# A gated linear recurrence and its feed-forward block on one core: the order of emission taken from a list schedule, early chunks transposed on TensorE, weights loaded in pieces

## The chip, the cores and the metric

The kernel runs on one core of a Trainium2 chip. The metric is the device time of one execution in microseconds (us); lower is better. The core's engines run their own instruction queues in order: TensorE (PE: matmuls, and transposes as matmuls against an identity), VectorE (DVE), ScalarE (ACT: tanh, exp, sqrt and copies), GpSimd (POOL) and SyncE (SP: here it only issues transfers). The matmuls write to PSUM, which DVE and ACT read.

## What is computed

```python
sig_r, sig_i = sigmoid(r_gate), sigmoid(i_gate)                  # x, gates: (4, 5824, 256)
a_t = exp(8 * sig_r * log(clip(sigmoid(a_param), 1e-6, 1 - 1e-6)))
x_gated = sqrt(max(1 - a_t * a_t, 1e-6)) * sig_i * x
for t in range(5824):                                            # a recurrence along the sequence
    h = a_t[:, t] * h + x_gated[:, t]
    y[:, t] = h
y = y.reshape(23296, 256)
out = (((y @ w1) * (y @ w2)) @ w3) @ w_out                       # w1, w2: 256x1024, w3: 1024x1024, w_out: 1024x256
```

All inputs and the output are float32; matmuls run in bf16.

## The kernel before

The 23296 tokens are cut into 46 chunks: chunk 0 of 256 tokens, the others of 512. A chunk passes through a front, a scan and the matmuls.

- The front. `load` fetches r, i and x of the chunk (256 columns of float32, tokens on partitions; three buffers for each of the three). `tanh_r` and `tanh_i` run on ACT (a sigmoid is a tanh of half the argument). POOL makes u from th_i and x (L106, L107). The recurrence needs the channels on partitions, so th_r and u are transposed as bf16 by `turn`: one DMA transpose on SP's queue (two for chunk 0), tiles rt and ut. `decay` (ACT, L125, twice a chunk, one for each half of the 256 channels) makes a_t as an exp, `square` (POOL, L131) its square, `root` (ACT, L136) the norm, `gated` (DVE, L144) the gated input.
- The scan. `scan` (DVE, L164, twice a chunk) runs the recurrence, with the last column of the chunk before as its start; `cast` (POOL, L170) makes y_t in bf16.
- The matmuls. `up` computes, for two of the eight blocks of 128 features at a time, pa with w1 and pb with w2 (four matmuls each; a pool of three PSUM tiles "pab"), ACT copies pa to sa, DVE multiplies sa by pb into g_t. w3 and w_out are multiplied once into wp_sb: `fold` loads 128 rows of w3 by POOL's queue, transposes them on TensorE (ptw), copies them (w3t), multiplies by wo (pw) and copies the result. `down` multiplies 128 tokens of g_t by wp_sb into po, ACT copies two of these to ot, SP stores them. ptw, pw and po share two PSUM tiles, "po".

A tanh or an exp needs one table on ACT, the square root another; a change of table is an ACT_TABLE_LOAD. So the chunks are put in groups (1, 1, 2, 3, nine times 4, and 3): the roots of a group stand together.

The order is written by hand as a loop over steps s, one chunk each, with four quarters. In a quarter stand one `up` of chunk s, one `down` of chunk s - 2, a piece of the scan of chunk s + 2, and the operations of the fronts that a table `queue` spreads over the steps ahead. The eight folds stand in steps 0 and 1. Weights: w1, w2 and wo are asked for whole at the start on POOL's queue, each w3 block where its fold stands. No instruction is reordered after this: each engine takes its own in the order of emission and waits for what it needs.

Of the kernel before, what the change touches and what calls it, by code (L numbers as in the profile page):

```python
# [1 line left out]

# [16 lines left out]
def kernel(  # L19
# [12 lines left out]
    nc = tc.nc  # L32
# [50 lines left out]
    def load(c):  # L83
        n = sizes[c] // P
        for nm, src in (("r", rf), ("i", jf), ("x", xf)):
            t = loads.tile([P, 4, D], F32, name=nm + "_t", tag=nm)
            nc.sync.dma_start(  # L87
                out=t[:, :n, :],
                in_=src[starts[c]:starts[c] + sizes[c], :].rearrange("(n p) c -> p n c", p=P))
            T[nm, c] = t  # L90

    def tanh_r(c):
        n = sizes[c] // P
        t = gates.tile([P, NCB, 4, P], BF16, name="th_r", tag="th_r")
        nc.scalar.activation(out=t[:, :, :n, :].rearrange("p cb j q -> p j cb q"),  # L95
                             in_=T["r", c][:, :n, :].rearrange("p j (cb q) -> p j cb q", q=P),
                             func=AF.Tanh, scale=0.5)
        T["pr", c] = turn(t, n, "rt")
        T["a", c] = held.tile([P, NCB, CT], F32, name="a_t", tag="a")

    def tanh_i(c):
        n = sizes[c] // P
        t = gates.tile([P, 4, D], F32, name="th_i", tag="th_i")
        nc.scalar.activation(out=t[:, :n, :], in_=T["i", c][:, :n, :], func=AF.Tanh, scale=0.5)  # L104
        u = gates.tile([P, NCB, 4, P], BF16, name="u_t", tag="u")
        nc.gpsimd.tensor_scalar(t[:, :n, :], t[:, :n, :], 1.0, 0.5, op0=ALU.add, op1=ALU.mult)  # L106
        nc.gpsimd.tensor_mul(out=u[:, :, :n, :].rearrange("p cb j q -> p j cb q"),  # L107
                             in0=t[:, :n, :].rearrange("p j (cb q) -> p j cb q", q=P),
                             in1=T["x", c][:, :n, :].rearrange("p j (cb q) -> p j cb q", q=P))
        T["u", c] = u  # L110

    def turn(src, n, tag):
        dst = (gates if tag == "rt" else held).tile([P, NCB, 4, P], BF16, name=tag, tag=tag)
        if n == 4:
            nc.sync.dma_start_transpose(out=dst.rearrange("p cb j q -> p (cb j) q"),
                                        in_=src.rearrange("p cb j q -> p (cb j q)"))
        else:
            for cb in range(NCB):
                nc.sync.dma_start_transpose(out=dst[:, cb, :n, :],
                                            in_=src[:, cb, :n, :].rearrange("p j q -> p (j q)"))  # L120
        return dst.rearrange("p cb j q -> p cb (j q)")

    def decay(c, cb):
        w = sizes[c]
        nc.scalar.activation(out=T["a", c][:, cb, :w], in_=T["pr", c][:, cb, :w], func=AF.Exp,  # L125
                             scale=la4[:, cb:cb + 1], bias=la4[:, cb:cb + 1])
# [41 lines left out]
    def cast(c):  # L168
        w = sizes[c]
        nc.gpsimd.tensor_copy(out=T["y", c][:, :, :w], in_=T["h", c][:, :, :w])  # L170

    def up(c, mp):
# [159 lines left out]
```

## Time and profile before

| | |
|---|---|
| median of 3 runs | 600.25 us (599.87 to 605.09) |
| profiled execution | 604.79 us, its span (first to last instruction) 602.9 us |
| PE, DVE, ACT, POOL busy | 503.1, 459.5, 460.2, 360.1 us |
| DMA transposes | 47 for rt, 47 for ut |
| bytes read from and written to HBM | 78.91 MB, 23.86 MB |

Times in profile rows are us from the start of the span, unless marked ns. A timeline row has start, duration, engine, line, operation, output<-input, and in brackets the idle time before it with what ended it; SPq is the issue of a transfer by SP. A row by stages has, behind its bounds, the busy us of PE, PE's weight loads, DVE, ACT and POOL with their instruction counts, then the clock granted to TensorE, the busy share of the DMA engines and GB/s. A row of waits has the total, the number and the longest. q0 is the queue of transfers issued by POOL, q1 that of SP. Matmuls overlap, so their starts tell the pace better than their durations.

### The profile page before, as it was taken

The numbers are of one execution on the slowest core, as the hardware profiler recorded it, in microseconds if no ns is written. First come the engines' busy times: TensorE is split into PE (matmuls) and PEld (weight loads), VectorE is DVE, ScalarE is ACT, GpSimd is POOL, SyncE is SP. The second block draws the span as 40 slices with busy tenths as digits, with TensorE's granted clock in tenths as the row PEclk, the third lists the DMA queues.
The fourth block names the chain that finished last, engine by engine and source line by source line (L and its number), as shares of the span: only waits on it lengthen the run. The fifth ranks groups of instructions, "written<-read, shape, count | busy, mean of one in ns | idle before, by whom it ended". The sixth has DMA issues, their size and how long they took to land.

```text
span 602.9 us, 8389 instructions
## 1 busy us (share of the span) xinstructions
PE 503.1 (83%) x3056; PEld 302.3 (50%) x3056; DVE 459.5 (76%) x347; ACT 460.2 (76%) x537; POOL 360.1 (60%) x201
## 2 busy tenths in 40 slices
PE   0010826888899999999999999999999999999997
PEld 0000513444455565565555556556555555665565
DVE  0120333699799899999998998998998998988741
ACT  3466142698979989899899899889899898785443
POOL 3065281289497596595794893993993974630100
PEclk9999975999999999999999999999999999999999
DMA  9979588088989799789789999887998988421113
GB/s 195 292 210 251 128 204 184 2 219 194 307 205 315 222 195 336 213 192 339 203 196 313 210 209 307 210 241 252 223 272 228 215 221 268 99 77 49 40 53 106
DMA packets 196090, 123.51 MB, mean 205 GB/s; under 512 B 100304, under 2 KB 194512, under 8 KB 196048
## 3 DMA queue, kind: packets, MB, share of 16 engines
q1 hardware_dynamic: 193312, 119.30, 73.6%
q0 software_dynamic: 2736, 3.67, 3.8%
q8 instruction: 24, 0.39, 0.3%
q14 instruction: 18, 0.15, 0.1%
HBM read 78.91 MB, written 23.86 MB: 170 GB/s over the span
## 4 chain that ended last, share of the span: by engine, by line
PE 55%; ACT 12%; issue 11%; DVE 7%; POOL 7%; DMA 5%; SPq 3%; ACTq 0%; POOLq 0%; DVEq 0%
PE po L197 18%; PE pa L178 18%; PE pb L186 17%; ACT sa L181 5%; DVE g_t L190 5%; ACT a_t L125 3%; SPq L87 3%; POOL nrm L131 3%; DMA rt<-th_r 2%; POOL u_t L107 2%; DVE h_t L164 1%; DMA w_t<-in_moe_w_dram 1%; POOL th_i L106 1%; ACT th_i L104 1%; PE pw L220 1%
## 5 line engine op out<-in xcount | busy, mean ns | idle before, releaser
L190 DVE TENSOR_TENSOR g_t<-sa,pb 128x1024 bf16<-128x1024 bf16 (+1 forms) x184 | 218.3, 1195 | 67.4 <-ACT sa L181 55.5
L181 ACT CAST sa<-pa 128x1024 bf16<-128x1024 f32 (+1 forms) x184 | 184.0, 1000 | 75.8 <-PE pa L178 74.3
L178 PE MATMUL pa<-y_t,w_sb 128*128 128x512 bf16 (+1 forms) x736 | 189.6, 381 | 49.3 <-POOL y_t L170 36.5
L186 PE MATMUL pb<-y_t,w_sb 128*128 128x512 bf16 (+1 forms) x736 | 189.4, 380 | 5.5 <-ACT sa L181 5.4
L197 PE MATMUL po<-wp_sb,g_t 128*128 128x256 bf16 x1456 | 187.4, 273 | 0.0
L164 DVE TENSOR_TENSOR_SCAN h_t<-a_t,h_t,nrm 128x512 f32<-128x512 f32 (+3 forms) x90 | 182.4, 2028 | 0.0
L197 PEld LDWEIGHTS <-g_t 128*128 128x128 bf16 x1456 | 142.5, 98 | 53.6
L131 POOL TENSOR_TENSOR nrm<-a_t 128x1024 f32<-128x1024 f32 (+1 forms) x46 | 111.3, 2421 | 26.6 <-ACT a_t L125 26.6
L106 POOL TENSOR_SCALAR th_i<-th_i 128x1024 f32<-128x1024 f32 (+1 forms) x46 | 71.8, 1560 | 91.8 <-ACT th_i L104 81.6
L178 PEld LDWEIGHTS <-w_sb 128*128 128x128 bf16 x736 | 72.6, 99 | 101.8 <-issue 44.9
L107 POOL TENSOR_TENSOR u_t<-th_i,x_t 128x1024 bf16<-128x1024 f32 (+1 forms) x46 | 116.7, 2537 | 5.9 <-DMA x_t<-in_x_dram 2.1
L186 PEld LDWEIGHTS <-w_sb 128*128 128x128 bf16 x736 | 72.8, 99 | 93.6 <-issue 9.6
L170 POOL CAST y_t<-h_t 128x1024 bf16<-128x1024 f32 (+1 forms) x46 | 56.2, 1221 | 81.6 <-DVE h_t L164 70.6
L125 ACT ACTIVATE a_t<-rt,la 128x512 f32<-128x512 bf16 (+1 forms) x92 | 70.8, 808 | 24.3 <-DMA rt<-th_r 24.3
L144 DVE SCALAR_TENSOR_TENSOR nrm<-nrm,ut 128x1024 f32<-128x1024 f32 (+1 forms) x46 | 62.4, 1357 | 29.9 <-ACT nrm L136 29.9
L204 ACT COPY ot<-po 128x512 f32<-128x512 f32 x91 | 52.8, 580 | 32.5 <-PE po L197 29.1
L136 ACT ACTIVATE nrm<-nrm 128x1024 f32<-128x1024 f32 (+1 forms) x46 | 48.2, 1051 | 2.8 <-POOL nrm L131 2.6
L104 ACT ACTIVATE th_i<-i_t 128x1024 f32<-128x1024 f32 (+1 forms) x46 | 48.4, 1052 | 1.7 <-DMA i_t<-in_i_gate_dram 1.7
L95 ACT ACTIVATE th_r<-r_t 128x1024 bf16<-128x1024 f32 (+1 forms) x46 | 48.4, 1053 | 0.2
L214 PE MATMUL ptw<-ident,w_t 128*128 128x128 bf16 x64 | 7.9, 298 | 34.3 <-DMA w_t<-in_moe_w_dram 34.3
L214 PEld LDWEIGHTS <-w_t 128*128 128x128 bf16 x64 | 6.7, 141 | 36.3 <-DMA w_t<-in_moe_w_dram 35.3
L220 PE MATMUL pw<-wo_sb,w3t 128*128 128x256 bf16 x64 | 13.4, 382 | 6.8 <-DVE w3t L217 6.8
(23 smaller groups left out, 69.5 us busy)
## 6 DMA issues: line engine op xcount, KB each, us to landing
out_dram<-ot SPq DMA_DIRECT2D x91, 256.0 KB, 3.1
r_t<-in_r_gate_dram SPq DMA_DIRECT2D x45, 512.0 KB, 4.3
i_t<-in_i_gate_dram SPq DMA_DIRECT2D x45, 512.0 KB, 5.4
x_t<-in_x_dram SPq DMA_DIRECT2D x45, 512.0 KB, 6.7
w_t<-in_moe_w_dram POOLq DMA_DIRECT2D x8, 256.0 KB, 5.5
w_sb<-in_moe_w_dram POOLq DMA_DIRECT2D x2, 512.0 KB, 8.0
rt<-th_r SPq DMA_TRANSPOSE x47, 3.1
ut<-u_t SPq DMA_TRANSPOSE x47, 4.0
```

The source lines that it names most:

```text
L106: nc.gpsimd.tensor_scalar(t[:, :n, :], t[:, :n, :], 1.0, 0.5, op0=ALU.add, op1=ALU.mult)
L107: nc.gpsimd.tensor_mul(out=u[:, :, :n, :].rearrange("p cb j q -> p j cb q"), in0=t[:, :n, :].rearrange("p j (cb q) -> p j cb q", q=P), in1 ...
L125: nc.scalar.activation(out=T["a", c][:, cb, :w], in_=T["pr", c][:, cb, :w], func=AF.Exp, scale=la4[:, cb:cb + 1], bias=la4[:, cb:cb + 1])
L131: nc.gpsimd.tensor_mul(out=t[:, :, :w], in0=T["a", c][:, :, :w], in1=T["a", c][:, :, :w])
L144: nc.vector.scalar_tensor_tensor(out=T["n", c][:, :, :w], in0=T["n", c][:, :, :w], scalar=1e-3, in1=T["pu", c][:, :, :w], op0=ALU.max, op1 ...
L164: nc.vector.tensor_tensor_scan(T["h", c][:, cb, lo:hi], T["a", c][:, cb, lo:hi], T["n", c][:, cb, lo:hi], init, ALU.mult, ALU.add)
L170: nc.gpsimd.tensor_copy(out=T["y", c][:, :, :w], in_=T["h", c][:, :, :w])
L178: nc.tensor.matmul(out=pa[:, q, :w], lhsT=w1_sb[:, cb, m * P:(m + 1) * P], rhs=T["y", c][:, cb, :w], start=(cb == 0), stop=(cb == NCB - 1))
L181: nc.scalar.copy(out=sa[:, :, :w], in_=pa[:, :, :w])
L186: nc.tensor.matmul(out=pb[:, q, :w], lhsT=w2_sb[:, cb, m * P:(m + 1) * P], rhs=T["y", c][:, cb, :w], start=(cb == 0), stop=(cb == NCB - 1))
L190: nc.vector.tensor_mul(out=T["g", c][:, 2 * mp:2 * mp + 2, :w], in0=sa[:, :, :w], in1=pb[:, :, :w])
L197: nc.tensor.matmul(out=T["po", c][:, j % 2, :], lhsT=T["g", c][:, k, j * P:(j + 1) * P], rhs=wp_sb[:, k, :], start=(k == 0), stop=(k == KD ...
```

## The change

The loop is replaced by a table of jobs, one for each call of a helper. Each has an engine, an assumed duration, a due time, the jobs it comes after, the pool it takes a buffer from, and the jobs that use the buffer. A list scheduler walks through time, gives each free engine the startable job with the earliest due time, counts buffers and a DMA backlog, and so gets a start time for every job. The jobs are then emitted in the order of these times. The times themselves are not in the program: as before, an instruction starts when its engine has done what stands ahead of it and its data and buffers are there.

With it come: groups of 2, 1, 1, 1, 2, 3 and then nine times 4 chunks; chunks 0 to 6 transposed on TensorE into "po" tiles of PSUM (`turn_pe`), from which decay and gated read; for chunks 0 to 2 `times` (which is then the whole of u) and `square` on DVE, for chunks 0 and 1 also `cast`; w1 and w2 loaded in eight pieces of 256 columns; a tile of its own for each of the eight w3 blocks, so that they need not wait for a buffer; la4 loaded by ACT's queue. The factor 0.5 of the sigmoid of i moves into the folded weight, where both factors of the product make it 0.25.

```diff
-    group_sizes = [1, 1, 2, 3] + [4] * 9 + [3]
+    group_sizes = [2, 1, 1, 1, 2, 3, 4, 4, 4, 4, 4, 4, 4, 4, 4]
...
+    NPE = 7
+    NDV = 3
+    NCV = 2
...
+        if c < NDV:
+            nc.vector.scalar_tensor_tensor(out=flat(u)[:, :n, :], in0=t[:, :n, :], scalar=1.0,
+                                           in1=T["x", c][:, :n, :], op0=ALU.add, op1=ALU.mult)
...
+    def turn_pe(c, key, nm):
+        n = sizes[c] // P
+        pt = psum_o.tile([P, NCB, CT], BF16, name="ptr", tag="po")
+        for cb in range(NCB):
+            for j in range(n):
+                nc.tensor.matmul(
+                    out=pt[:, cb, j * P:(j + 1) * P],
+                    lhsT=flat(T[nm, c])[:, j, cb * P:(cb + 1) * P], rhs=ident,
+                    is_transpose=True,
+                    start=(cb == 0 and j == 0), stop=(cb == NCB - 1 and j == n - 1))
+        T[key, c] = pt
...
+    def load_w(mp, w_sb, w_in):
+        cols = slice(2 * mp * P, 2 * (mp + 1) * P)
+        nc.gpsimd.dma_start(out=w_sb[:, :, cols], in_=w_in.rearrange("(cb p) f -> p cb f", p=P)[:, :, cols])
...
+    def load_w3(mi):
+        T["w3", mi] = consts.tile([P, DFF], BF16, name="w3_t", tag="w3_%d" % mi)
+        nc.gpsimd.dma_start(out=T["w3", mi], in_=moe_w3[mi * P:(mi + 1) * P, :])
...
+        nc.vector.tensor_scalar(wp_sb[:, mi, :], T["pw", mi], 0.25, None, op0=ALU.mult)
...
+                job(("scan", c, cb), "DVE", 0.2 + 1.4 * f, U - D_SCAN + 1.5 * cb, partial(scan, c, cb),
...
+    for _, _, key in sorted(order):
+        if jobs[key]["fn"]:
+            jobs[key]["fn"]()
```

Three places show what becomes of the order at the start. DVE before, its first rows (la is the decay constant, ident the identity that TensorE's transposes need, nrm the norm, h_t the scan):

```order
L268 TENSOR_SCALAR la_86<-la_86 128x2
L269 TENSOR_SCALAR la_86<-la_86 128x2
L71 CAST ident<-ident_f 128x128
L144 SCALAR_TENSOR_TENSOR nrm<-nrm,ut 128x2x256
L164 SCALAR_TENSOR_TENSOR h_t<-a_t,nrm 128x256 x2
```

DVE now, from the same place to the scans of chunk 1:

```order
L470 TENSOR_SCALAR la_86<-la_86 128x2
L137 SCALAR_TENSOR_TENSOR u_t<-th_i,x_t 128x512
L73 CAST ident<-ident_f 128x128
L175 TENSOR_TENSOR nrm<-a_t 128x2x256
L137 SCALAR_TENSOR_TENSOR u_t<-th_i,x_t 128x1024
L175 TENSOR_TENSOR nrm<-a_t 128x1024
L185 SCALAR_TENSOR_TENSOR nrm<-nrm,ptr 128x2x256
L200 SCALAR_TENSOR_TENSOR h_t<-a_t,nrm 128x256 x2
L185 SCALAR_TENSOR_TENSOR nrm<-nrm,ptr 128x1024
L208 CAST y_t<-h_t 128x2x256
L200 SCALAR_TENSOR_TENSOR h_t<-a_t,h_t,nrm 128x512 x2
```

The products and squares of chunks 0 and 1 have come to DVE, the cast of the identity stands behind the first of them, and the gated input of chunk 1 ahead of the cast of chunk 0.

POOL before, from the cast of chunk 0 to the first loads of w3 (numbers tell the chunks apart):

```order
L170 CAST y_t_146<-h_t_145 128x2x256
L106 TENSOR_SCALAR th_i_187<-th_i_187 128x1024
L107 TENSOR_TENSOR u_t_189<-th_i_187,x_t_113 128x4x2x128
L106 TENSOR_SCALAR th_i_198<-th_i_198 128x1024
L107 TENSOR_TENSOR u_t_200<-th_i_198,x_t_142 128x4x2x128
L131 TENSOR_TENSOR nrm_214<-a_t_186 128x1024
L131 TENSOR_TENSOR nrm_220<-a_t_197 128x1024
L170 CAST y_t_181<-h_t_180 128x1024
L211 DMA w3_t_239<-in_moe_w3_dram 128x1024
L211 DMA w3_t_262<-in_moe_w3_dram 128x1024
```

POOL now, from the identity to its first work for chunks 2 and 3 (w_sb are the pieces of w1 and w2, w_t the blocks of w3):

```order
masks.py:199 AFFINE_SELECT ident_f<-ident_f 128x128
L252 DMA w_sb<-in_moe_w_dram 128x2x256 x7
L255 DMA wo_sb<-in_moe_w_out_dram 128x8x256
L259 DMA w_t<-in_moe_w_dram 128x1024 x6
L175 TENSOR_TENSOR nrm<-a_t 128x1024
L259 DMA w_t<-in_moe_w_dram 128x1024 x2
L130 TENSOR_SCALAR th_i<-th_i 128x1024
L208 CAST y_t<-h_t 128x1024
L140 TENSOR_TENSOR u_t<-th_i,x_t 128x1024
```

Six of the eight w3 blocks stand ahead of all of POOL's computing; its first own operation is the square of chunk 3, its first cast that of chunk 2.

ACT before, from the first tanh to the fronts of chunk 1:

```order
L95 ACTIVATE th_r<-r_t 128x2x2x128
L104 ACTIVATE th_i<-i_t 128x512
L125 ACTIVATE a_t<-rt,la_86 128x256 x2
L136 ACT_TABLE_LOAD
L136 ACTIVATE nrm<-nrm 128x2x256
L95 ACT_TABLE_LOAD
L95 ACTIVATE th_r<-r_t 128x4x2x128
L104 ACTIVATE th_i<-i_t 128x1024
L125 ACTIVATE a_t<-rt,la_86 128x512 x2
```

ACT now, from the first tanh to the first copies:

```order
L116 ACTIVATE th_r<-r_t 128x512
L125 ACTIVATE th_i<-i_t 128x512
L168 ACTIVATE a_t<-ptr,la_86 128x256 x2
L116 ACTIVATE th_r<-r_t 128x1024
L125 ACTIVATE th_i<-i_t 128x1024
L168 ACTIVATE a_t<-ptr,la_86 128x512 x2
L180 ACT_TABLE_LOAD
L180 ACTIVATE nrm<-nrm 128x2x256
L180 ACTIVATE nrm<-nrm 128x1024
L116 ACT_TABLE_LOAD
L116 ACTIVATE th_r<-r_t 128x1024
L125 ACTIVATE th_i<-i_t 128x1024
```

Chunks 0 and 1 are one group now: the root of chunk 0 stands behind both tanh and both decays of chunk 1, and the decays read PSUM (ptr).

More of the change, by code (lines that the diff above doesn't have):

```diff
@@ L110, in tanh_i @@
-        T["u", c] = u
[L112 to L121, printed above, removed]
+        T["thi", c] = t
@@ L182, in up, with product @@
[L182 to L187 removed]
+        nc.scalar.copy(out=sa[:, :, :w], in_=T["pa", c, mp][:, :, :w])
+        T["sa", c, mp] = sa
+    def product(c, mp):
+        w = sizes[c]
         if mp == 0:
@@ L266 @@
+    nc.scalar.dma_start(out=la4, in_=a_param.rearrange("(cb p) -> p cb", p=P))
     nc.scalar.activation(out=la4, in_=la4, func=AF.Exp, scale=-1.0)
```

368 lines of the change are left out of this document (247 added, 121 removed).

## The prediction

> **What bounds the kernel now.** I first cut the span at the places where its pace changes; the list of stages gives the busy time of each engine (PE, weight loads, DVE, ACT, POOL), then the granted clock.
>
> ```profile
> 0.00:59.10 59.10, 1.87 (x8) 1.11 (x8) 6.80 (x10) 30.80 (x34) 24.68 (x25) 1.00 0.93 237
> 59.10:120.40 61.30, 39.70 (x220) 24.87 (x221) 25.13 (x31) 21.88 (x26) 22.00 (x17) 0.83 0.60 131
> 120.40:201.50 81.10, 72.64 (x430) 41.74 (x430) 73.47 (x50) 73.00 (x87) 63.38 (x31) 1.00 0.93 250
> 201.50:555.60 354.10, 345.55 (x2113) 206.55 (x2112) 330.56 (x238) 313.37 (x367) 247.96 (x126) 1.00 0.82 220
> 555.60:602.90 47.30, 43.35 (x288) 27.98 (x286) 23.55 (x20) 21.19 (x26) 2.08 (x2) 1.00 0.20 68
> ```
>
> TensorE is nearly idle for 59 us, half idle or slow for 61 more, and from 201.5 on it is 97.6% busy. The copies of finished half chunks (two to a chunk of 512 tokens) give the pace:
>
> ```profile
> L204 ACT COPY ot<-po x14: 567/585/599, 120.4 to 201.5; 128x512 f32<-128x512 f32 x14
> L204 ACT COPY ot<-po x67: 566/585/588, 201.5 to 555.6; 128x512 f32<-128x512 f32 x67
> ```
>
> Thirteen intervals, 6.5 chunks, take 81.1 us: 12.5 us a chunk. Then 66 intervals, 33 chunks, take 354.1 us: 10.73 us a chunk. What TensorE alone needs is read near the end, where the other engines have little left:
>
> ```profile
> 569.26 1.03 PE L186 MATMUL pb<-y_t,w_sb 128*128 128x512 bf16 x4
> 571.87 1.03 PE L186 MATMUL pb<-y_t,w_sb 128*128 128x512 bf16 x4
> 590.93 8.02 PE L197 MATMUL po<-wp_sb,g_t 128*128 128x256 bf16 x72
> ```
>
> A quarter chunk (one pa, one pb, one down) takes 2.61 us, a chunk 10.4, and the last matmul ends at 598.95, 3.95 before the end of the span. So the steady part can give only 33 x 0.33 = 11 us; what is large lies ahead of 201.5. There the waits, in total, number and longest, say:
>
> ```profile
> PE pa L178 <- POOL y_t L170: 36.5, 1, 36.5
> PE ptw L214 <- DMA w_t<-in_moe_w_dram: 34.3, 2, 20.8
> ACT a_t L125 <- DMA rt<-th_r: 24.3, 4, 15.0
> ```
>
> The timeline shows how they come about:
>
> ```profile
> 8.26 0.63 ACT L104 ACTIVATE th_i<-i_t 128x512 f32<-128x512 f32 x1 [1.70 <-DMA i_t<-in_i_gate_dram]
> 11.71 1.26 POOL L107 TENSOR_TENSOR u_t<-th_i,x_t 128x512 bf16<-128x512 f32 x1 [2.12 <-DMA x_t<-in_x_dram]
> 15.71 4.11 SPq L119 DMA_TRANSPOSE rt<-th_r  x2
> ...
> 23.91 1.09 ACT L125 ACTIVATE a_t<-rt,la 128x256 f32<-128x256 bf16 x2 [15.03 <-DMA rt<-th_r]
> 25.02 1.28 ACT L136 ACT_TABLE_LOAD   x1
> 26.32 0.63 ACT L136 ACTIVATE nrm<-nrm 128x512 f32<-128x512 f32 x1
> 26.98 0.69 DVE L144 SCALAR_TENSOR_TENSOR nrm<-nrm,ut 128x512 f32<-128x512 f32 x1 [21.83 <-ACT nrm L136]
> 27.71 1.27 DVE L164 TENSOR_TENSOR_SCAN h_t<-a_t,nrm 128x256 f32<-128x256 f32 x2
> ...
> 55.26 1.18 POOL L211 DMA_DIRECT2D w_t<-in_moe_w_dram  x2
> ```
>
> The tanh of chunk 0's r, ahead of that of i, is done before 8.3; its transpose issues at 15.7 behind nine loads, and the decay that needs it starts at 23.9; and the first W3 rows are asked for at 55.3, because POOL's queue has the cast of chunk 1 ahead of them, so folding starts at 59.1.
>
> **The change: the first up.** Loads keep their order on SP; la4 moves to ACT's queue, so they issue 0.5 us earlier. Until 18.0 (wo issued at 3.28 plus 14.7) before's weights compete with them, and the new pieces and W3 rows do so likewise, since POOL has no compute ahead of them; so I keep before's landings, less 0.5. The issues, then the queues and the times from issue to landing of the first 10 us:
>
> ```profile
> 3.28 0.90 POOL L262 DMA_DIRECT2D wo_sb<-in_moe_w_out_dram  x1
> 3.30 0.96 SPq L87 DMA_DIRECT2D i_t<-in_i_gate_dram  x1
> 4.30 3.43 SPq L87 DMA_DIRECT2D x_t<-in_x_dram  x1
> ...
> q0 software_dynamic: 471, 0.93, 53.3%
> q1 hardware_dynamic: 1020, 0.73, 28.1%
> ...
> wo_sb<-in_moe_w_out_dram POOLq DMA_DIRECT2D x1, 512.0 KB, 14.7
> i_t<-in_i_gate_dram SPq DMA_DIRECT2D x1, 512.0 KB, 14.3
> x_t<-in_x_dram SPq DMA_DIRECT2D x1, 512.0 KB, 14.7
> ```
>
> Chunk 1's i and x, issued at 3.30 and 4.30, land at 17.6 and 19.0; now 17.1 and 18.5. Chunk 0's x came by 11.7 (u_t above), now 11.2. The new DVE order puts the ident cast behind times(0), which needs that x. Behind the cast waits TensorE's first transpose, behind that ACT's decay(0), and behind that tanh_r(1): 11.2 + 0.69 (L144's 128x512) + 0.2 for the cast = 12.1; four slow transposes (half of the 1.06 us quoted below) bring it to 12.6, two decays (1.09) to 13.7. This wait hides: tanh_i(1) cannot start before 17.1 anyway. From there: tanh_i(1) 1.06 to 18.2, two decays 1.6 to 19.8, table 1.28 to 21.1, root(0) 0.63 to 21.7. DVE has by then done times(1) and square(1), about 1.2 each from 18.5 (an estimate from 0.69 for half the size). Gated(0) 0.7, scans 1.27, gated(1) 1.2, which stands ahead of cast(0), and the cast, about 0.5, estimated from the same 0.69: the first up at **25.4** instead of 36.5. Bounds: 22 if i(1) is not late (decays from 16 on); 33 if SP moves only what q1 moved here, 0.73 MB in some 7.6 us after a start near 2.4, so that chunks 0 and 1 (2.36 MB) are complete near 27 instead of 18.5.
>
> A page of the Trainium skill speaks against pieces and more queues: "DMA: Bandwidth & Descriptors", section Rules for kernel authors, wants small transfers coalesced and says that queues share the same engines. The q0 and q1 rows agree on the sharing; the pieces would cost nothing by my row, as nobody waits for w1 before 25, and up to the 8 us of the upper bound by the rule of the Trainium skill.
>
> **TensorE from there on**, by rows that show fast and slow groups:
>
> ```profile
> 74.90 1.06 PE L178 MATMUL pa<-y_t,w_sb 128*128 128x256 bf16 x4
> 75.75 1.06 PE L186 MATMUL pb<-y_t,w_sb 128*128 128x256 bf16 x4
> ...
> 96.82 1.06 PE L214 MATMUL ptw<-ident,w_t 128*128 128x128 bf16 x8
> 98.67 1.89 PE L220 MATMUL pw<-wo_sb,w3t 128*128 128x256 bf16 x8 [0.79 <-DVE w3t L217]
> ...
> 106.84 0.61 PE L214 MATMUL ptw<-ident,w_t 128*128 128x128 bf16 x8
> 108.24 1.05 PE L220 MATMUL pw<-wo_sb,w3t 128*128 128x256 bf16 x8 [0.79 <-DVE w3t L217]
> ```
>
> - Chunks: 45.5 x 10.4 = 473.2 (as before).
> - Folds: 8 x (0.61 + 1.05) = 13.3. Their W3 rows are issued early (wo and W3 each wait for the landing of the weight transfer eight before), so the 34.3 us of waiting go. The last two stand behind square(3) on POOL, and so do plus(3) and cast(2); I put that among the ramp waits.
> - Transposes: 14, four of them ahead of the first up; 10 x 0.61 = 6.1. A trade: 16 DMA transposes go from SP's queue (the two quoted above held it for 4.1 us).
> - Slow clock: groups of four 128x256 matmuls run 0.85 apart, twice the fast pace, until TensorE has worked without a gap. Chunk 0's eight groups: 8 x 0.43 = 3.4.
> - Ramp waits, which no row shows directly. ACT must feed TensorE and at the same time build a lead of about three chunks:
>
> ```profile
> L125 ACT ACTIVATE a_t<-rt,la 128x512 f32<-128x512 bf16 x90 | 69.7, 813 | 9.3 <-DMA rt<-th_r 9.3
> L104 ACT ACTIVATE th_i<-i_t 128x1024 f32<-128x1024 f32 x45 | 47.8, 1061 | 0.0
> L136 ACT ACT_TABLE_LOAD x14 | 18.0, 1283 | 0.2
> ```
>
>  A front (two tanh and a root at about 1.06, two decays at 0.81) is 4.8 us, three are 14.4; five small groups cost 10 table loads (12.8) where shares of large groups would be 5. So 22 us extra, against 19.4 in which TensorE folds and transposes without ACT. By the sum nearly 0; by the nearest row, before's ramp, 6.5 chunks lost 81.1 - 67.6 = 13.5. Again DMA-bound gates, a table switch per group, PSUM's two "po" tiles (now shared by transposes, folds and downs), and POOL are in that row, so I take **13**; 0 and 30 (twice the row and a little) are the ends.
> - Steady: the same 33 x 0.33 = 11; DVE, ACT and POOL do the same work per chunk in another order. Ends 0 and 25.
> - End: 4.0.
>
> Sum: 25.4 + 473.2 + 13.3 + 6.1 + 3.4 + 13 + 11 + 4.0 = **549.4 us of span**. The profiled execution took 604.79, 1.9 over its span, and 4.5 over the median of the runs: 551.3 on the first reckoning, 546.8 on the second. I take **549**. A measurement of this kernel cannot tell differences under 1% from none.
>
> DVE's operations for chunks 0 to 2 (times, square; cast for 0 and 1) come to about 7.5 us by the same estimates; DVE waits for loads until 25 and they take POOL off the path; if DVE were the bound in the ramp they would count in full, which the 30 covers.
>
> **Rivals.**
> 1. *The early chunks starve TensorE* (chance 0.15). Each small group is a serial chain: load, tanh, transpose, decay, square, switch, root, gate, scan. For: in 59 to 120 TensorE was busy 39.7 of 61.3 with such groups. Against: 21 us of that were W3 waits. If the ramp loses 30 and the first up comes 5 late: 549 + 17 + 5 = 571.
> 2. *The slow clock lasts* (0.10). The rows at 59 to 76 mix transposes and matmuls with gaps and stay slow; if chunk 1's ups (8 x 0.86) and the folds (8 x 0.84) are slow as well, 549 + 13.6 = 563. The Trainium skill, "TensorE: Matmul & The Clock Gate", Part 4, says that transposes do not count as work for the clock; by that rule this case would hold, and the rows at 74.9 and 98.67 do not exclude it.
> 3. *A frozen order misfits the real durations: slower than before* (0.04). The planner takes 1.6 us for a scan; measured, with POOL beside it:
>
> ```profile
> L164 DVE TENSOR_TENSOR_SCAN h_t<-a_t,h_t,nrm 128x512 f32<-128x512 f32 x84 | 173.9, 2072 | 0.0
> ```
>
>  With two scans DVE is 0.9 us a chunk over plan, and in order, so products behind a scan hold PSUM and TensorE. At 0.9 over 43 chunks, 39 us: 588, still faster. From 1.2 us a chunk lost (51 / 43) it is slower; a full scan lost each chunk, 2.07 x 43 = 89, gives 638. Against: DVE was 93% busy at before's pace with the same scans, and the tail has slack.
> 4. *The pieces fill the queues* and the first up comes at 33, all else as summed (0.08): 557. Here the change does not do what its due times say, since no due time holds an instruction back.
> 5. *The order is better everywhere* (0.08): ramp waits and steady losses at their lower ends, 549 - 24 = 525.
>
> **How the numbers follow.** The forecast keeps 0.55, with 538 to 562 for itself. To hold 8 in 10 the range takes in rivals 1, 2 and 4 and leaves out 3 and most of 5: 535 to 576. Faster by over 1%: 0.95; within 1%: 0.02 (rival 3 with a misfit near 1.2 us a chunk); slower: 0.03.
>
> **What would show it.** In the changed profile: the first pa near 25, behind gated(1) and cast(0); the ident cast after times(0), near 12; no wait of ptw on W3 over 1 us; groups of four 128x256 matmuls 0.85 apart in chunk 0; the copy of chunk 7's first half, at 201.5 before, near 150; intervals of 10.7 us a chunk after that. I am wrong if the span from that copy to the end grows beyond the 401 us of before (then the new order costs in the steady part), or if chunk 7 comes out after 175 (then the ramp).

## The result and the profile after

The changed kernel takes 574.81 us (median of 4 runs, 573.72 to 575.35), before 600.69 beside it (4 runs, 599.87 to 605.09): a ratio of 0.9553, 95% interval 0.9504 to 0.9601. The forecast was 549, the range 535 to 576: the direction is right, the time is at the range's upper end. That it lies inside the range is partly luck: the upper end was set for rivals 1, 2 and 4, none of which happened, and the loss that did happen, 32.5 us in the steady part, is beyond the 25 us that the forecast gave that term at most. The profiled execution took 574.65 us, its span is 572.9.

By stages of the changed kernel (busy us of PE, weight loads, DVE, ACT, POOL, then the granted clock), cut at the first up, the first finished copy, and the copies of chunk 7's first half and, 34 chunks later, of chunk 41's:

```profile
0.00:20.20 20.20, 3.08 (x24) 2.49 (x25) 7.87 (x13) 15.01 (x18) 10.73 (x21) 1.00 1.06 237
20.20:63.76 43.56, 36.44 (x288) 24.99 (x288) 32.95 (x38) 30.61 (x36) 16.98 (x12) 0.96 0.88 235
63.76:141.50 77.74, 68.82 (x439) 41.13 (x438) 57.11 (x43) 73.08 (x86) 59.23 (x34) 1.00 0.97 258
141.50:529.10 387.60, 355.13 (x2159) 209.94 (x2158) 341.83 (x244) 324.92 (x381) 231.45 (x128) 1.00 0.79 213
529.10:572.90 43.80, 39.81 (x256) 24.82 (x254) 23.55 (x20) 19.98 (x24) 3.97 (x3) 1.00 0.18 60
```

PE is idle for 7.1 and 8.9 us in the two stages after the first up, for 32.5 us in the long one, for 4.0 at the end. With 20.2 ahead of the first up and 500.2 of work (20.2 + 500.2 + 7.1 + 8.9 + 32.5 + 4.0) that is the span. The copies of half chunks, in the kernel before and then in the changed one:

```profile
L204 ACT COPY ot<-po x69: 566/585/588, 201.5 to 566.0; 128x512 f32<-128x512 f32 x69
```

```profile
L243 ACT COPY ot<-po x69: 563/586/616, 141.5 to 529.1; 128x512 f32<-128x512 f32 x69
```

The first of these 69 is chunk 7's: 60 us earlier than before. But the 68 intervals, 34 chunks, take 387.6 us instead of 364.5: **11.40 us a chunk instead of 10.72**. From that copy to the end of the span it is 431.4 instead of 401.4: half of what the start gained is given back. The start, from its timeline (in this and the later timelines, rows of other engines are left out at "..."):

```profile
9.28 0.22 DVE L73 CAST ident<-ident_f 128x128 bf16<-128x128 f32 x1
9.55 0.58 PE L150 MATMUL ptr<-ident,th_r 128*128 128x128 bf16 x4 [9.55 <-DVE ident L73]
...
12.04 1.05 ACT L125 ACTIVATE th_i<-i_t 128x1024 f32<-128x1024 f32 x1
...
14.44 1.23 DVE L137 SCALAR_TENSOR_TENSOR u_t<-th_i,x_t 128x1024 bf16<-128x1024 f32 x1 [2.52 <-DMA x_t<-in_x_dram]
...
20.21 1.01 PE L216 MATMUL pa<-y_t,w_sb 128*128 128x256 bf16 x4 [3.46 <-DVE y_t L208]
21.02 1.06 PE L216 MATMUL pb<-y_t,w_sb 128*128 128x256 bf16 x4
...
25.29 0.60 PE L216 MATMUL pa<-y_t,w_sb 128*128 128x256 bf16 x4
25.72 0.60 PE L216 MATMUL pb<-y_t,w_sb 128*128 128x256 bf16 x4
...
33.51 1.03 PE L216 MATMUL pb<-y_t,w_sb 128*128 128x512 bf16 x4
34.37 1.03 PE L216 MATMUL pa<-y_t,w_sb 128*128 128x512 bf16 x4
```

Chunk 1's i is used at 12.04 and its x at 14.44, the first pa stands at 20.21 (36.5 before). Groups of four 128x256 start 0.81 apart there and 0.43 apart from 25; chunk 1's, of 128x512, 0.86 apart. In the long stage one wait of PE has grown. The largest of PE's waits from 200 to 480, before and then after, is this:

```profile
PE pa L178 <- DVE g_t L190: 7.3, 12, 1.1
```

```profile
PE pa L216 <- DVE g_t L230: 23.7, 22, 1.9
```

PE waits for products of DVE (they free the PSUM tiles of pa and pb). Why DVE is late is seen in the timelines of DVE and POOL, side by side:

```profile
303.64 3.31 DVE L200 TENSOR_TENSOR_SCAN h_t<-a_t,h_t,nrm 128x512 f32<-128x512 f32 x1
306.88 1.19 DVE L230 TENSOR_TENSOR g_t<-sa,pb 128x1024 bf16<-128x1024 bf16 x1
307.99 1.27 DVE L200 TENSOR_TENSOR_SCAN h_t<-a_t,h_t,nrm 128x512 f32<-128x512 f32 x1
309.18 1.19 DVE L230 TENSOR_TENSOR g_t<-sa,pb 128x1024 bf16<-128x1024 bf16 x1
310.30 3.32 DVE L200 TENSOR_TENSOR_SCAN h_t<-a_t,h_t,nrm 128x512 f32<-128x512 f32 x1
```

```profile
303.52 2.35 POOL L142 TENSOR_TENSOR u_t<-th_i,x_t 128x1024 bf16<-128x1024 f32 x1
307.09 1.04 POOL L208 CAST y_t<-h_t 128x1024 bf16<-128x1024 f32 x1 [1.21 <-DVE h_t L200]
308.09 2.01 POOL L130 TENSOR_SCALAR th_i<-th_i 128x1024 f32<-128x1024 f32 x1
310.19 2.35 POOL L142 TENSOR_TENSOR u_t<-th_i,x_t 128x1024 bf16<-128x1024 f32 x1
```

A scan takes 1.27 us when POOL is not at work as it starts; the scans of 303.64 and 310.30 start 0.1 behind an operation of POOL of 2.35 and last until 1.1 after its end. The other way round, POOL's th_i of 308.09 takes 2.01 as the scan of 307.99 is running. Of the 45 scans of 128x512 that start from 200 to 480, the 13 that find POOL idle take 1.27 to 1.28 us; the 32 that start while POOL is at work all end 1.07 to 1.14 us after the end of its operation. The shortest, median and longest (ns) of each kind from 200 to 500 say whom this concerns:

```profile
L185 DVE SCALAR_TENSOR_TENSOR nrm<-nrm,ut x26: 1212/1222/3329, 200.6 to 484.1; 128x1024 f32<-128x1024 f32 x26
L230 DVE TENSOR_TENSOR g_t<-sa,pb x103: 1187/1198/1223, 199.5 to 497.8; 128x1024 bf16<-128x1024 bf16 x103
L130 POOL TENSOR_SCALAR th_i<-th_i x26: 1043/1836/2014, 201.1 to 490.2; 128x1024 f32<-128x1024 f32 x26
L142 POOL TENSOR_TENSOR u_t<-th_i,x_t x26: 2348/2354/3137, 202.8 to 492.2; 128x1024 bf16<-128x1024 f32 x26
L175 POOL TENSOR_TENSOR nrm<-a_t x26: 1887/1894/2871, 205.9 to 499.6; 128x1024 f32<-128x1024 f32 x26
L208 POOL CAST y_t<-h_t x26: 1027/1037/2040, 209.0 to 495.7; 128x1024 bf16<-128x1024 f32 x26
```

Gates are stretched like scans, products never: of DVE's three, the product alone reads an operand from PSUM. The early chunks show the same within one operation: up to chunk 6 the gate reads the transposed u from PSUM (ptr), later from SBUF (ut), the on-chip memory of all the other tiles. The gates of 128x1024 from 20 to 145, with the mean in ns behind the busy time:

```profile
L185 DVE SCALAR_TENSOR_TENSOR nrm<-nrm,ut 128x1024 f32<-128x1024 f32 x4 | 6.8, 1709 | 2.3 <-ACT nrm L180 2.3
L185 DVE SCALAR_TENSOR_TENSOR nrm<-nrm,ptr 128x1024 f32<-128x1024 f32 x5 | 6.1, 1217 | 4.6 <-ACT nrm L180 4.6
```

Three of the five with ptr start while POOL is at work (at 71.17, 81.87 and 88.86) and take 1.21 to 1.22 us all the same. By the shortest times a chunk has 2 x 1.27 + 1.21 = 3.8 us of scans and gate and 1.04 + 2.35 + 1.89 + 1.03 = 6.3 of POOL that exclude each other: 10.1 of TensorE's 10.4 us. The Trainium skill, "SBUF — State Buffer", section "SBUF: two separate sides", states such a lock on the pair of ports that DVE and GpSimd share, also for DVE operations with two inputs in SBUF; these rows agree.

Both orders collide: scans of 128x512 from 200 to 480, with gates, before and then after (the mean, in ns, is behind the busy time):

```profile
L164 DVE TENSOR_TENSOR_SCAN h_t<-a_t,h_t,nrm 128x512 f32<-128x512 f32 x46 | 101.6, 2209 | 0.0
L144 DVE SCALAR_TENSOR_TENSOR nrm<-nrm,ut 128x1024 f32<-128x1024 f32 x27 | 36.3, 1344 | 0.0
```

```profile
L200 DVE TENSOR_TENSOR_SCAN h_t<-a_t,h_t,nrm 128x512 f32<-128x512 f32 x45 | 97.9, 2175 | 0.3
L185 DVE SCALAR_TENSOR_TENSOR nrm<-nrm,ut 128x1024 f32<-128x1024 f32 x25 | 40.1, 1602 | 7.1 <-ACT nrm L180 7.1
```

So the scans have not become longer (the gates have, by 0.26 us). What differs is what stands behind them. DVE's order in the steady part (G a gate, S a scan, P a product), one chunk before, a group of four chunks after:

```
before  G P S P S P P
after   G S P P G S P G P S P S P G P S P S P S P S P P P P P P
```

Before, three quarters of a gate or scan stand to each product: 1.20 + 0.75 x 1.92 (the mean of two scans and a gate) = 2.64 us a product, beside the 2.6 that TensorE needs. After, a stretch of 12 gates and scans with 10 products takes 10 x 1.20 + 12 x 1.98 = 35.8 us where TensorE needs 26; the six products that follow could be quick, but by then TensorE has waited, with only three PSUM tiles to run ahead on. This reckoning is from means; the runs below bear it out only in part.

### The profile page after: what moved, and what is told of

The parts are those of the page before. It is cut to its first block, busy times and chain, and to the rows that moved or that the text cites. A ratio compares the mean times of both kernels' runs of the same rounds, so it can differ in the third digit from the quotient of the medians.

```text
span 572.9 us, 8556 instructions
## 1 busy us (share of the span) xinstructions
PE 503.3 (88%) x3160; PEld 303.4 (53%) x3160; DVE 463.3 (81%) x355; ACT 463.6 (81%) x539; POOL 322.4 (56%) x196
## 4 chain that ended last, share of the span: by engine, by line
PE 58%; DVE 22%; issue 7%; ACT 7%; DMA 5%; POOL 0%; SPq 0%; DVEq 0%; ACTq 0%; POOLq 0%
PE pa L216 20%; PE pb L216 19%; PE po L237 18%; DVE h_t L200 11%; DVE g_t L230 8%; DMA r_t<-in_r_gate_dram 4%; ACT sa L223 2%; DVE nrm L185 1%; ACT a_t L168 1%; ACT nrm L180 1%; ACT L180 1%; DMA la<-in_a_param_dram 1%; ACT th_r L118 1%; ACT ot L243 1%; PE pw L275 0%
## 5 line engine op out<-in xcount | busy, mean ns | idle before, releaser
L216 PE MATMUL pa<-y_t,w_sb 128*128 128x512 bf16 (+1 forms) x736 | 188.8, 379 | 41.8 <-DVE g_t L230 34.3
L237 PE MATMUL po<-wp_sb,g_t 128*128 128x256 bf16 x1456 | 182.5, 273 | 2.0 <-ACT ot L243 2.0
L200 DVE TENSOR_TENSOR_SCAN h_t<-a_t,h_t,nrm 128x512 f32<-128x512 f32 (+3 forms) x90 | 169.7, 1892 | 0.8
L175 POOL TENSOR_TENSOR nrm<-a_t 128x1024 f32<-128x1024 f32 x43 | 89.3, 2079 | 55.1 <-ACT a_t L168 55.1
L208 POOL CAST y_t<-h_t 128x1024 bf16<-128x1024 f32 x44 | 53.4, 1213 | 109.0 <-DVE h_t L200 107.8
L142 POOL TENSOR_TENSOR u_t<-th_i,x_t 128x1024 bf16<-128x1024 f32 x39 | 95.0, 2436 | 3.0
L130 POOL TENSOR_SCALAR th_i<-th_i 128x1024 f32<-128x1024 f32 x43 | 65.6, 1527 | 48.3 <-ACT th_i L125 48.2
L185 DVE SCALAR_TENSOR_TENSOR nrm<-nrm,ut 128x1024 f32<-128x1024 f32 x39 | 62.1, 1598 | 13.3 <-ACT nrm L180 13.3
L243 ACT COPY ot<-po 128x512 f32<-128x512 f32 x91 | 53.2, 585 | 14.6 <-PE po L237 14.4
L168 ACT ACTIVATE a_t<-rt,la 128x512 f32<-128x512 bf16 x78 | 61.8, 814 | 1.7 <-DMA rt<-th_r 1.6
L118 ACT ACTIVATE th_r<-r_t 128x1024 bf16<-128x1024 f32 x39 | 41.3, 1062 | 0.0
L150 PE MATMUL ptr<-ident,th_r 128*128 128x128 bf16 x52 | 5.3, 260 | 15.4 <-DVE ident L73 9.6
```

The source lines that it names most:

```text
L130: nc.gpsimd.tensor_scalar(t, t, 1.0, 1.0, op0=ALU.add, op1=ALU.mult)
L142: nc.gpsimd.tensor_mul(out=u.rearrange("p cb j q -> p j cb q"), in0=cut(t), in1=cut(T["x", c]))
L175: eng.tensor_mul(out=t[:, :, :w], in0=T["a", c][:, :, :w], in1=T["a", c][:, :, :w])
L185: nc.vector.scalar_tensor_tensor(out=T["n", c][:, :, :w], in0=T["n", c][:, :, :w], scalar=1e-3, in1=T["pu", c][:, :, :w], op0=ALU.max, op1 ...
L200: nc.vector.tensor_tensor_scan(T["h", c][:, cb, lo:hi], T["a", c][:, cb, lo:hi], T["n", c][:, cb, lo:hi], init, ALU.mult, ALU.add)
L216: nc.tensor.matmul(out=pp[:, q, :w], lhsT=w_sb[:, cb, m * P:(m + 1) * P], rhs=T["y", c][:, cb, :w], start=(cb == 0), stop=(cb == NCB - 1))
```

## The experiments

**Theory A**: gates and scans of DVE and POOL's operations exclude each other, and the new order turns that into waits of TensorE. **Rivals**: the order alone (bunched gates and scans; B), the planner's short durations, and for the start the pieces (C), the transposes, the W3 rows. The letters in an expectation are those of that run alone: its theory B or rival D is said there. All kernels in one table; the copy is that of chunk 7's first half, the pace is over the 34 chunks behind it, the scan is the mean of 128x512 from 200 to 480.

| kernel | us | ratio to before (95%) | copy at | us a chunk | scan, ns |
|---|---|---|---|---|---|
| before | 600 to 604 | 1 | 201.5 | 10.72 | 2209 |
| after | 574.81 | 0.9553 (0.9504 to 0.9601) | 141.5 | 11.40 | 2175 |
| e1 after, POOL thinned | 536.12 | 0.8878 (0.8825 to 0.8932) | 140.0 | 10.32 | 1384 |
| e5 before, POOL thinned | 593.29 | 0.9805 (0.9746 to 0.9864) | 200.2 | 10.40 | 1381 |
| e2 spread | 566.20 | 0.9377 (0.9340 to 0.9414) | 143.7 | 10.95 | 2122 |
| e3 spread, longer durations | 567.11 | 0.9365 (0.9305 to 0.9424) | 144.0 | 11.23 | 2096 |
| e9 planner excludes | 568.83 | 0.9414 (0.9374 to 0.9455) | 147.0 | 11.11 | 1761 |
| e7 scans write y | 550.39 | 0.9107 (0.9084 to 0.9129) | 135.3 | 10.83 | 1776 |
| e8 scans write y, spread | 561.46 | 0.9287 (0.9268 to 0.9307) | 134.5 | 11.24 | 1980 |
| e10 scans write y, planner excludes | 545.61 | 0.9031 (0.8989 to 0.9073) | 133.3 | 10.88 | 1824 |
| e12 and half of u on DVE | 536.41 | 0.8905 (0.8856 to 0.8954) | 133.0 | 10.57 | 1560 |
| e4 whole weights | 578.43 | 0.9579 (0.9543 to 0.9616) | 145.2 | 11.40 | 2126 |
| e6 DMA transposes | 590.84 | 0.9765 (0.9733 to 0.9797) | 159.2 | 11.28 | 1972 |
| e11 late W3 | 579.63 | 0.9595 (0.9553 to 0.9636) | 141.6 | 11.54 | 2187 |

**POOL's work, with the order kept (e1, e5).** From chunk 14 on u and the norm are made in part only, in tiles that an earlier chunk has used, so the rest of them is stale and the output is not the reference's. The edit of e1 (that of e5 does the same to the kernel before):

```diff
...
-            nc.gpsimd.tensor_mul(out=u.rearrange("p cb j q -> p j cb q"), in0=cut(t), in1=cut(T["x", c]))
+            k = P if c < 14 else 8
+            nc.gpsimd.tensor_mul(out=u.rearrange("p cb j q -> p j cb q")[:, :, :, :k], in0=cut(t)[:, :, :, :k],
+                                 in1=cut(T["x", c])[:, :, :, :k])
...
-        eng.tensor_mul(out=t[:, :, :w], in0=T["a", c][:, :, :w], in1=T["a", c][:, :, :w])
+        k = w if c < 14 else 32
+        eng.tensor_mul(out=t[:, :, :k], in0=T["a", c][:, :, :k], in1=T["a", c][:, :, :k])
```

> The changed kernel with its order untouched, but from chunk 14 on GpSimd's two long operations work on a small part only (u on 8 of each 128 columns, the square on 32 of 512 tokens), so part of u and of the norm is stale. The changed kernel takes 574.8 us and gives a chunk every 11.40 us from 141.5 on. Theory A (scans and gates on VectorE are stretched while these two GpSimd operations run, 2.16 us a scan instead of 1.28, and where the new order puts two of them ahead of a product, TensorE waits): scans near 1.3 us, TensorE's waits for the product nearly gone, 10.4 to 10.7 us a chunk, 548 to 553 us. Theory B (the order itself starves TensorE through ScalarE's roots, tables and copies): scans get shorter but the pace stays at 11.2 to 11.4, 569 to 575 us.

> The kernel before, with POOL's work thinned in the same way as in e1: from chunk 14 on u is made on 8 of each 128 columns and the square on 32 of 512 tokens, so the output is not the reference's; order, waits and all other engines' work are unchanged. Theory A (POOL operations and DVE's gates and scans cannot run side by side, and the new order only makes it cost more): the old order pays a little of it too. Its pace from chunk 14 on falls from 10.73 to about 10.4 us a chunk, some 31 chunks x 0.33 = 10 us: 590 to 595 beside 600 to 603, so that the two orders differ in what the exclusion costs them (0.33 against about 1.0 us a chunk). Rival B (the old order's steady loss has other causes, such as the copies or the PSUM tiles): 600 to 603, although scans become shorter.

The changed kernel drops to 536.12, more than theory A expected, the old one to 593.29 (0.98 of its time), as expected. Their stages from 200 to 480, e1 and then e5:

```profile
200.00:300.00 100.00, 100.00 (x615) 60.07 (x614) 83.54 (x71) 91.24 (x109) 32.48 (x40) 1.00 0.93 238
```

```profile
200.00:480.00 280.00, 278.28 (x1690) 168.18 (x1722) 228.46 (x195) 262.16 (x311) 88.49 (x111) 1.00 0.98 249
```

TensorE is busy throughout in both, and no wait of PE for a product is left in either from 200 to 480. With POOL thinned the two orders have one pace (10.32 and 10.40); with POOL whole they differ by 0.68 us a chunk. So the loss is neither the new order's alone nor POOL's alone: POOL's work costs the old order 0.3 and the new one 1.1 us a chunk. (DVE's own work was kept. POOL's two operations also end sooner and move less, which these runs cannot tell apart from the exclusion; but from 200 to 480 the changed kernel's DVE has no wait for POOL that this could shorten, only 7.1 us for ACT's root and 23.2 for the copies and matmuls ahead of products.)

**The order, with the work kept (e2, e3, e9).** The rule of e2 in the planner, and the durations that e3 adds:

```diff
+            if key[0] in ("gated", "scan") and key[1] >= 8 and t < gap[0]:
+                continue
...
+            if key[0] in ("gated", "scan"):
+                gap[0] = free[e] + GAP
+                heapq.heappush(events, gap[0])
+            elif key[0] == "product":
+                gap[0] = 0.0
...
-                    job(("scan", c, cb), "DVE", 0.2 + 1.4 * f, ...
+                    job(("scan", c, cb), "DVE", 0.2 + 1.9 * f, ...
```

> The changed kernel, with one rule added to its scheduler: from chunk 8 on no second gate or scan is started on VectorE within 3 us of the last one unless a product came between. All work is done. In the changed order 22 of the stretches between two products hold two or three gates or scans, before's order has 6. Theory A (pairs ahead of a product make TensorE wait): the pace falls from 11.40 to 10.7 to 10.9 us a chunk, 552 to 560 us. Rival (the stretched operations cost as much wherever they stand, since VectorE's sum is what counts): 570 to 576 us.

> As the run with the rule, and the planner also takes a scan at 2.1 us and a gate at 1.6 (measured 2.16 and 1.67) instead of 1.6 and 1.25. Pairs are as few, but the long runs of six or seven products with no gate or scan between, in which VectorE waits, are gone too. Theory A: 10.6 to 10.8 us a chunk, 548 to 556 us, no more than 5 under the run with the rule alone. Rival (sum of VectorE): 570 to 576 us.

e2 gains 8.6 us, about half of what was expected; the wait for products falls to 16.0 us (16 times). e3 adds nothing that can be seen (567.11, its four runs from 562.23 to 568.04): a planner with the longer mean durations still puts scans where POOL is at work (2096 ns). For e9 the planner keeps the two apart:

```diff
+            if uses_port(key) and port[0] > t + 1e-6:
+                continue
...
+        return key[0] in ("gated", "scan", "square", "times", "plus", "cast")
```

> The changed kernel with a planner that knows the exclusion: a gate or scan of DVE (and its square, times and cast of the early chunks) and any compute operation of POOL may not overlap in the plan, each with the time that it takes alone in the trace (scan 1.28, gate 1.22, POOL 1.05 to 2.35). Same instructions, another order. Theory A, if a frozen order can dodge collisions: scans of 1.5 to 1.8 instead of 2.15 us, 555 to 566. Theory B (the exclusion is there, but DVE and POOL drift against the plan, so that no frozen order can dodge it): scans still near 2.1, and since the plan has 10.1 us of exclusive work to fit beside products it puts products behind it: 570 to 585.

```profile
L200 DVE TENSOR_TENSOR_SCAN h_t<-a_t,h_t,nrm x50: 452/1277/3377, 199.8 to 475.9; 128x512 f32<-128x512 f32 x46, 128x128 f32<-128x128 f32 x2, 128x320 f32<-128x320 f32 x2
```

The median scan of e9 is 1277 ns: more than half now run free, so a frozen order can dodge collisions in part, against theory B. The time is that of e2 all the same, between the two forecasts. From 147.0 to 524.8 TensorE is idle for 17.4 us, where the changed kernel had 32.5 and e2 22.8; but chunk 7 comes 5.5 us later, and for 10 us of this stretch the granted clock is half:

```profile
303.70:307.10 3.40, 3.40 (x10) 1.20 (x9) 2.59 (x3) 1.72 (x2) 1.66 (x2) 0.50 1.12 337
412.90:419.80 6.90, 4.59 (x11) 1.54 (x11) 6.44 (x7) 6.01 (x8) 4.33 (x4) 0.51 1.17 296
```

At half pace that is about 4 us (an estimate: half of TensorE's 8.0 busy us in the two rows), which e2 does not lose there. DVE also has runs of up to nine gates and scans, and 10.1 us of exclusive work leave little room for good places; how much of the time is due to that was not separated.

**Less work that excludes (e7, e8, e10, e12).** In e7 the scans write y_t, and POOL's cast is gone:

```diff
-                init = T["h", c - 1][:, cb, pw - 1:pw]
+                init = T["y", c - 1][:, cb, pw - 1:pw]
...
-                T["h", c][:, cb, lo:hi], T["a", c][:, cb, lo:hi], T["n", c][:, cb, lo:hi],
+                T["y", c][:, cb, lo:hi], T["a", c][:, cb, lo:hi], T["n", c][:, cb, lo:hi],
```

> The changed kernel with POOL's cast taken away: the scans write the bf16 y tile themselves, and the next chunk's scan starts from y's last column (rounded to bf16). Theory A: what cannot overlap falls from 10.1 to 9.1 us a chunk, so the excess over TensorE's 10.4 falls from 1.0 to 0.3 to 0.6 us a chunk; with 45 casts gone from the chain of the early chunks as well, 552 to 563. Rival (the losses come from the bunched order of DVE's own work, whatever POOL does): the order stays bunched, so 570 to 575, less 1 to 2 for the start.

> e7 with e2's rule in the planner: from chunk 8 on no second gate or scan within 3 us of the last unless a product stands between. If bunching and exclusion are two factors of one loss (theory A): it is the fastest of the versions that compute all, 545 to 555, pace 10.5 to 10.7 us a chunk. If e7 has already taken all that POOL costs, the rule adds nothing: within 3 us of e7.

e7 takes 550.39, 24 us less, better than expected: 6.2 at chunk 7, the rest in the pace. Its order is made anew but stays bunched, with up to five products on end in the steady part. e8 refutes its expectation: the rule that helped e2 costs 11 us here, and scans grow from 1776 to 1980 ns. Not more of them meet POOL (from 200 to 480, 37 of 49 scans of 128x512 start while POOL is at work in e7, 30 of 45 in e8), but those that do take longer, 2.29 us instead of 1.91 in the mean; why is open. So bunching is not by itself the fault, and e2's rule is not to be carried over.

> e7 (scans write y, no cast on POOL) with e9's planner. Theory A: exclusive work of 9.1 us a chunk, dodged by plan: 541 to 548, scans under 1.6 us. Theory B: within 3 us of e7 or slower, 548 to 562, scans at e7's 1.78 or above.

e10 (e7 with e9's planner) is 545.61, in theory A's range; but the pace is e7's (10.88 and 10.83), and its scans are 1824, as theory B had it. Of the 3.8 us between the two profiled spans, 2.0 are gained ahead of chunk 7's copy and 3.5 behind that of chunk 41, and 1.7 are lost between them. In e12 DVE makes u of every second chunk:

```diff
+        elif on_dve(c):
+            for cb in range(NCB):
+                q = slice(cb * P, (cb + 1) * P)
+                nc.vector.scalar_tensor_tensor(out=u[:, cb, :, :], in0=t[:, :, q], scalar=1.0,
+                                               in1=T["x", c][:, :, q], op0=ALU.add, op1=ALU.mult)
```

> e10 with the u of every second chunk from chunk 12 on made by DVE (two operations of half a chunk, about 0.65 us each, which also add the 1) instead of by POOL (1.04 + 2.35). Theory A: what cannot overlap falls from 9.1 to 8.0 us a chunk (3.8 + 0.65 on DVE, 1.7 + 1.87 on POOL), the pace from 10.88 to 10.5 to 10.7: 534 to 542, scans under 1.7 us. Rival: DVE's own load is what counts (products 4.8, scans and gate 3.8, now 0.65 more, 9.3 of 10.4 us), and work that waits for loads stands in its queue ahead of products: 547 to 556.

```profile
200.00:300.00 100.00, 97.65 (x597) 57.99 (x595) 88.69 (x76) 92.38 (x111) 40.89 (x22) 1.00 1.00 264
300.00:400.00 100.00, 100.00 (x614) 59.99 (x613) 91.44 (x81) 95.74 (x110) 35.01 (x17) 1.00 0.99 256
400.00:500.00 100.00, 100.00 (x614) 59.95 (x613) 90.88 (x78) 84.31 (x99) 32.27 (x16) 1.00 0.55 144
```

536.41, as theory A said: DVE has more work and TensorE waits less. Wherever the exclusive work was cut, the time fell: from 10.1 to 9.1 us a chunk between the changed kernel and e7, e2 and e8, e9 and e10 (by 24.4, 4.7 and 23.2 us), from 9.1 to 8.0 between e10 and e12 (9.2 us). The pace does not follow this sum alone: at 10.1 it is 10.72 in the kernel before and 10.95 to 11.54 in the new orders, at 9.1 it is 10.83 (e7), 10.88 (e10) and 11.24 (e8), at 8.0 10.57. What makes one order pay more than another for the same sum stays open. e12 computes all (only the state handed from chunk to chunk is rounded to bf16) and is the fastest version that does: 10.9% less than before, and by the two ratios (0.8905 and 0.9553) 6.8% less than the changed kernel.

**The start (e4, e6, e11).** e4 loads w1 and w2 each in one transfer:

```diff
-        cols = slice(2 * mp * P, 2 * (mp + 1) * P)
+        if mp:
+            return
+        cols = slice(0, DFF)
```

> The changed kernel with w1 and w2 loaded whole by one transfer each, where their first pieces stood; the emitted order is otherwise the same. In the changed kernel chunk 1's x was there at 14.4 us and the first up began at 20.2; I had forecast 18.5 and 25.4 by the landings of before. Theory C (the pieces and the wait of each later weight transfer for one eight before hold the weight queue back, and the loads get ahead): x of chunk 1 lands at 17 to 19, the first up starts at 23 to 26, and the time is 3 to 6 us longer, 578 to 581. Rival D (loads were early because nothing else is asked of SP's queue, such as the transposes of before): first up at 20 to 21, 574 to 576 us.

```profile
21.94 1.23 DVE L137 SCALAR_TENSOR_TENSOR u_t<-th_i,x_t 128x1024 bf16<-128x1024 f32 x1 [9.28 <-DMA x_t<-in_x_dram]
```

```profile
27.71 1.01 PE L216 MATMUL pa<-y_t,w_sb 128*128 128x256 bf16 x4 [3.45 <-DVE y_t L208]
```

Without the pieces chunk 1's x is used 7.5 us later, the first up comes 7.5 later, and the time is 3.6 more: the time that theory C expected, with the start later than its 23 to 26. The queues of the first 10 us say why; after, then e4:

```profile
q1 hardware_dynamic: 1777, 1.75, 58.3%
q0 software_dynamic: 785, 0.38, 27.9%
```

```profile
q0 software_dynamic: 419, 0.83, 46.1%
q1 hardware_dynamic: 932, 0.91, 35.6%
```

With eight pieces on the way, the W3 rows each wait for a piece to land, and the loads of the chunks get the engines. Whether it is the pieces' size or only this wait was not separated.

```diff
-    NPE = 7
+    NPE = 1
```

> The change with one part undone: chunks 1 to 6 are transposed by DMA as before, only chunk 0 on TensorE; the planner makes its order anew for that. If the transposes on TensorE carry the gain of the ramp: each early chunk gets back a DMA round of 3 to 4 us between tanh and decay, for six chunks in part hidden, so the copy of chunk 7's first half comes at 150 to 158 instead of 141.5, and the time is 583 to 592. If the gain is that of the order and the early loads and W3 rows alone: 573 to 577, or 2 to 4 less, since twelve groups of transposes (12 x 0.61 = 7) leave TensorE.

(In e6 u of chunks 1 and 2 stays in the layout for TensorE, so their part of the output differs; the work is the same.) The decay of chunk 1 waits for its transpose:

```profile
23.46 1.52 ACT L168 ACTIVATE a_t<-rt,la 128x512 f32<-128x512 bf16 x2 [10.56 <-DMA rt<-th_r]
```

The first up comes at 31.96 and chunk 7's copy at 159.2, just beyond the 150 to 158 expected for transposes that carry the gain; the 16 us lost (590.84) are as expected for them. Behind this DMA transpose in the crowded start the decay waits not 3 to 4 us but 10.56. The order was made anew as well, so how much of the 16 us is that of the transposes alone was not separated.

```diff
-        job(("w3", mi), "POOL", 0.8, DUE_W3 + 0.1 * mi, partial(load_w3, mi), mb=0.52)
+        job(("w3", mi), "POOL", 0.8, DUE_W3 + 0.1 * mi, partial(load_w3, mi), [("cast", 2)], mb=0.52)
```

> The changed kernel with the loads of the W3 rows planned behind the cast of chunk 2, as they stood behind the cast of chunk 1 before. If the early W3 rows matter to the ramp: the folds come some 10 us later, nothing can go down before them, products fill g's three buffers and TensorE waits: the first finished copy at 72 to 76 instead of 63.8, chunk 7's first half at 146 to 152, 579 to 586. If other work of the early chunks fills the time: 573 to 577.

The first copy comes at 71.2 instead of 63.8, yet chunk 7's is not late (141.6): the early work fills the gap. The time is 579.63; the 4.8 us lost lie behind that copy (11.54 us a chunk), in an order that the planner made anew; which part of it costs them stays open.

## Why the prediction was right or wrong

| term | forecast | measured | how |
|---|---|---|---|
| first up | 25.4 | 20.2 | timeline |
| work (chunks, folds, transposes, slow clock) | 496.0 | 500.2 | PE busy behind 20.2 |
| ramp waits | 13 | 16.0 | PE idle, 20.2 to 141.5 |
| steady | 11 | 32.5 | PE idle, 141.5 to 529.1 |
| end | 4.0 | 4.0 | PE idle behind 529.1 |
| span | 549.4 | 572.9 | |

- **First up: too late by 5.2.** The failed step is "so I keep before's landings": x of chunk 1 was there at 14.4, not 18.5, and i by 12.04, not 17.1. The weights took 0.38 MB of the first 10 us, not 0.93; with 0.83 (e4) the start is 7.5 us later. The chain behind the loads was sized well: from tanh_i(1) to the first up 17.1 to 25.4 forecast, 12.04 to 20.21 measured. It is not the upper bound of 33, nor rival 4. The rule of the Trainium skill, "DMA: Bandwidth & Descriptors", Rules for kernel authors, to coalesce small transfers, would have cost 7.5 us at the first up here, as e4 measured; that queues share the engines agrees with e4, where 0.83 MB of weights left 0.91 MB for the loads, against 0.38 and 1.75.
- **The ident cast** stands behind times(0), at 9.28. It does not hide behind the load of i(1) as reckoned, since tanh_i(1) starts right behind tanh_r(1); it costs little, because DVE, which waits for x(1) until 14.44, comes free for gated(0) no sooner than ACT's root(0) ends (16.7 both).
- **Slow clock: right in kind, priced on the high side for chunk 0.** Its first three groups run at the slow pace (0.81 to 0.85 apart), not all eight, and again one at 31.05 and the first of chunk 1, after TensorE stood idle up to 30.2; the rest of chunk 1 runs at 0.86 a group of 128x512, the fast pace. Rival 2 did not happen. The Trainium skill, "TensorE: Matmul & The Clock Gate", Part 4, says that transposes do not count as work for the clock; here eight of them stand at 22.72 among the slow groups, and the groups are fast from 23.38 until that idle time.
- **Work: 4.2 us over the sum.** About 2 of them are in the chunks (355.13 / 34 = 10.45 us instead of 10.4); the rest was not located.
- **Folds and W3: right in size**, since the 34.3 us of waits for W3 are gone; but e11, with the rows asked for later and chunk 7 no later, shows that other chunks' work fills such a gap: asking for the rows late cost 4.8 us in all, not 34, and those lie behind chunk 7, in an order made anew.
- **Transposes: priced right as a cost (0.61 each), not seen as a gain.** Chunk 7 came at 141.5, 8.5 earlier than forecast, of which 5.2 are the first up's; with most of them given back to the DMA queue, and an order made anew, it comes 17.7 us later (e6).
- **Steady: the step that failed.** "DVE, ACT and POOL do the same work per chunk in another order", with 11 us and ends of 0 and 25, measured 32.5. The work is the same, but a scan or gate that meets POOL's work delays the products behind it, and with POOL thinned the loss is gone (e1). That the new order loses more by it because it puts more gates and scans to each product for 2.5 chunks on end is argued from means; e2 bears it out by half, e8 speaks against it. The prediction's own test, the span from chunk 7's copy growing beyond 401 (431.4), told it. Even before's 0.33 a chunk was the same loss: without POOL's work it is gone (e5).
- **Rival 3** had the place (a frozen order, products behind stretched scans) and a chance of 0.04 for the wrong end: it was held to "slower than before". Its own 0.9 us a chunk gave 588, an outcome without a chance of its own; 0.7 was measured (11.40 less 10.72). Whether the planner's short scan, which it named as the cause, had a part is open: longer durations changed nothing on top of e2's rule (e3) and were not tried alone. The row it quoted, 2072 ns a scan beside 1.27 for chunk 0's two halves, already held the cause.

## What to carry to other kernels

Before an order is changed, look at the shortest and the longest of each operation, not only the mean: where they differ by 2.6 times, find the engine that excludes it, and add up the time that both need to themselves per step; here 10.1 of 10.4 us. Cutting that sum paid each time (e7, e12, and e8 and e10 against e2 and e9); moving the same work about gained 5 to 9 us in four versions (e2, e3, e9, e10) and lost 11 in a fifth (e8). A mean per chunk does not show what a new order costs: before and after have nearly the same mean scan (2209 and 2175 ns), and a pace of 10.72 and 11.40.

## What the runs showed of the hardware

- A scan or gate of DVE that meets an operation of POOL waits until that ends: 1.27 becomes up to 3.37 us, a gate 1.21 up to 3.33; POOL's wait for DVE likewise (1.04 to 2.01). Products with an operand in PSUM stay within 1.19 to 1.22, and so do the early gates that read the transposed u from PSUM (1.22 in the mean; those from SBUF in the same stretch 1.71).
- A scan that writes bf16 takes as long alone as one that writes float32: those of e10 that find POOL idle take 1.25 to 1.28 us, those of the changed kernel 1.27 to 1.28.
- Eight smaller weight transfers in place of two put the chunks' loads ahead: 1.75 instead of 0.91 MB of them in the first 10 us.
